# The last output tile of a gated attention and MLP kernel: two engines for its scaling, two queues for its stores

## The chip, the core and the metric

The kernel runs on one core of a Trainium2 chip. The metric is the device time of one execution in microseconds. A profile's span, from the first to the last instruction, is slightly shorter than the time of the same execution (268.4 us where the time was 270.24 us). The engines are TensorE (PE; PEld is its weight load), VectorE (DVE), ScalarE (ACT), GpSimd (POOL) and SyncE (SP). SPq and ACTq are the sequencers of SyncE and ScalarE, where DMAs are issued.

In this text, **tail** is the time from the end of the last matmul to the end of the span, and **relative times** ("at -0.43 us") are counted from the end of that last matmul. Both are read from the trace's instruction and semaphore records, which are finer than the rounded lines of the views.

## The reference

Two branches work on the same input x of 2048 x 512 (bfloat16), and a sigmoid gate per row mixes them:

```python
g = sigmoid((x * gate_w).sum(-1, keepdims=True))
a = attention_with_memory(x, wq, wk, wv, beta) @ wo    # 32 heads, 4 segments of 512 rows
h = gelu(x @ w_gate) * (x @ w_up)                       # 512 -> 1792
b = h @ w_down                                          # 1792 -> 512
return g * a + (1 - g) * b
```

## The kernel before

The kernel has a list scheduler of its own that orders all tasks on the engines before anything is emitted. Only the end matters here. The output is made in tiles of 128 rows x 512 columns. For each tile TensorE adds up the MLP part (`wdn`) and the attention part (`wo`) in one PSUM bank, one engine scales it by a factor per row into an SBUF buffer, and a DMA stores that buffer. The buffers come from a ring, `osb`, of two. The very last tile is cut in two column groups so that the last piece of work after TensorE is small: 384 columns first (in a buffer of the same ring), then 128 columns (in a buffer of its own, `ose`).

```python
RINGS = {..., "osb": 2, "ose": 1}
...
def out_group(s, qt, prio, cols=slice(0, D)):
    part = (cols.stop - cols.start) / D
    ring = "osb" if part > 1 / 4 else "ose"
    ...                                    # TensorE: 14 steps of wdn, 4 of wo
    def fo(e):
        bx["o"] = rtile(ring, [P, D if ring == "osb" else P])
        f = omz[:, s, qt:qt + 1]
        if e == "ACT":
            nc.scalar.activation(bx["o"][:, oc], bank(first)[:, cols], AF.Copy, scale=f)
        else:
            nc.vector.tensor_scalar_mul(bx["o"][:, oc], bank(first)[:, cols], f)
    ev = add(["DVE", "ACT"], [130 + 530 * part, 155 + 430 * part], fo, deps=[g, TAB["omz"]],
             alloc=[ring], frees=[("gen", first)])
    add("SP", 600, lambda _: nc.sync.dma_start(out2[q0:q0 + P, cols], bx["o"][:, oc]),
        deps=[ev], frees=[(ring, ev)], lat=2000)
...
for qt in range(KT - 1):                                       # three whole tiles
    out_group(NSEG - 1, qt, 9000 + qt)
for h, cols in enumerate((slice(0, 3 * P), slice(3 * P, D))):  # 384, then 128 columns
    out_group(NSEG - 1, KT - 1, 9010 + h, cols)
```

The scheduler chose ScalarE for all of the last four tiles. So the 384-column group takes the buffer that the tile two before it used, and has to wait until that tile's store has landed.

The softmax here doesn't subtract the row's maximum and nothing guards it: scores larger than these inputs give would overflow.

Of the kernel before, what the change touches and what calls it, by code (L numbers as in the profile page):

```python
# [13 lines left out]
P = 128  # L14
# [45 lines left out]
class Sched:  # L60
# [15 lines left out]
    def add(self, engs, cost, fn, **kw):  # L76

        if "PE" in engs and 0 < kw["prio"] < 9000:
            kw["prio"] += (ord(next(self.shift, "M")) - ord("M")) / 2
        engs = {engs: cost} if isinstance(engs, str) else dict(zip(engs, cost))  # L80
        t = Task(engs, fn, **kw)
        t.seq = len(self.tasks)
        self.tasks.append(t)
        return t
# [207 lines left out]
def kernel(  # L292
# [15 lines left out]
    nc = tc.nc  # L308
    assert tuple(A_x.shape) == (1, NSEG * L, D)
    x2 = A_x[0]  # L310
    out2 = out[0]
# [17 lines left out]
    add = S.add  # L329

    def ctile(name, shape, dtype=BF):
        return cp.tile(shape, dtype, name=name, tag=name)
# [10 lines left out]
    def bank(t, i=0):  # L343
        return banks(t, "gen", i)[:, 0, :]
# [4 lines left out]
    def rtile(ring, shape, dtype=BF, pool=None):  # L349
        pool = pool or (pools["wp"] if ring in WP else rp)  # L350
        return pool.tile(shape, dtype, name=ring, tag=ring, bufs=RINGS[ring])
# [21 lines left out]
    omz = ctile("omz", [P, NSEG, KT], F32)  # L373
# [86 lines left out]
    def group(name, cost, mms, prio, deps, alloc="gen", also=None, **kw):  # L460

        box = {}

        def fn(e):
            box["t"] = pair(t) if alloc == "pair" else bank(t)
            if also:
                also[1]()
            mms(box["t"])
        t = add("PE", cost, fn, prio=prio, deps=deps, alloc=[alloc] + ([also[0]] if also else []),
                **kw)  # L470
        return t, box
# [19 lines left out]
    def dense(t, lhsT, rhs, start, stop):  # L491


        if not tiled:
            nc.tensor.matmul(t, lhsT=lhsT, rhs=rhs, start=start, stop=stop)  # L495
            return
        for j in range(4):
            a = slice(32 * j, 32 * j + 32)
            nc.tensor.matmul(t[a, :], lhsT=lhsT[:, a], rhs=rhs, start=start, stop=stop,  # L499
                             tile_position=(0, 32 * j), skip_group_check=True)  # L500
# [141 lines left out]
    TAB = {}  # L642
# [100 lines left out]
    for s in range(NSEG):  # L743
        for hp in range(HS // 2):
            gate_pair(s, hp, -959 + 20 * s + hp)
            if s == 1 and hp == HS // 2 - 1:
                g, box = group("bps", 60, f_bps, -922, [a_be])
# [299 lines left out]
    def out_group(s, qt, prio, cols=slice(0, D)):  # L1047


        late = s == NSEG - 1  # L1050
        att = [t_wo] + [OTT[(s, c)] for c in range(NCH)]
        part = (cols.stop - cols.start) / D
        ring = "osb" if part > 1 / 4 else "ose"
        oc = cols if ring == "osb" else slice(0, P)
        q0 = s * L + qt * P
        prev = first = None
        for lo in range(0, HS, 2):
            def fn(_, lo=lo):
                for hs in (lo, lo + 1):
                    dense(bank(first)[:, cols], G[:, s, hs, qt * P:(qt + 1) * P], wdn[:, hs, cols],  # L1060
                          hs == 0, False)
            prev = add("PE", 2 * MM * part, fn, prio=prio, mode="more" if lo else "open",
                       deps=[prev] if lo else [UPT[(s, hs)] for hs in range(HS)] + [TAB["wdn"]]
                       + ([] if late else att[:ATT]), alloc=[] if lo else ["gen"], final=late)
            first = first or prev

        def fn_o(_):
            for c in range(NCH):
                dense(bank(first)[:, cols], xT[:, c, q0:q0 + P], wo[:, c, cols], False,
                      c == NCH - 1)  # L1070
        g = add("PE", 4 * MM * part, fn_o, prio=prio, deps=[prev] + att, final=late, mode="more")
        bx = {}
# [5 lines that stand above are left out]
                nc.scalar.activation(bx["o"][:, oc], bank(first)[:, cols], AF.Copy, scale=f)  # L1078
            else:
                nc.vector.tensor_scalar_mul(bx["o"][:, oc], bank(first)[:, cols], f)  # L1080
        ev = add(["DVE", "ACT"], [130 + 530 * part, 155 + 430 * part], fo, deps=[g, TAB["omz"]],
                 alloc=[ring], frees=[("gen", first)])
        add("SP", 600, lambda _: nc.sync.dma_start(out2[q0:q0 + P, cols], bx["o"][:, oc]),
            deps=[ev], frees=[(ring, ev)], lat=2000)

    TAB["first_x"] = None
# [4 lines left out]
    def fillers(s):  # L1091


        AE = ["DVE", "ACT"]
        n0 = NSLOT * s
        n1 = n0 + NSLOT
        if s > 0:
            mem_den(s, n0 + 2)
            for gp in range(2):
                mem_num(s, gp, n0 + 3 + 4 * gp)  # L1100
        ph = 2.5
        if s < NSEG - 1:
            phi_k(s, 0, ph)
            for pr in range(2):
                for which in "kq":
                    for c in (2 * pr, 2 * pr + 1):
                        qk_group(s + 1, c, which, n1 - 10 + 1.5 * c, AE)
                phi_q(s + 1, pr, ph)
                if pr == 0:
                    phi_k(s, 1, ph)  # L1110
            for i in range(KT):
                v_group(s + 1, i, n1 - 3, AE)
            for pr in range(2):
                m_update(s, pr, n1 - 8 + 5 * pr)
        for i, x in enumerate(UPS[s]):
            up_group(*x, n0 + 4 + 16 * (i + 1) / len(UPS[s]))
        if s > 0:
            for qt in range(KT):
                out_group(s - 1, qt, n0 + 5 * qt + 5)
# [12 lines left out]
    for qt in range(KT - 1):  # L1132
        out_group(NSEG - 1, qt, 9000 + qt)
    for h, cols in enumerate((slice(0, 3 * P), slice(3 * P, D))):
        out_group(NSEG - 1, KT - 1, 9010 + h, cols)
# [30 lines left out]
```

## Time and profile before

The time was 269.78 us, the median of three runs (269.45 to 270.19). From the page of the profile before: the span, the busy time of each engine with its share of the span, and the chain of waits by engine.

```profile
span 268.4 us, 10277 instructions
## 1 busy us (share of the span) xinstructions
PE 263.8 (98%) x4546; PEld 126.0 (47%) x4546; DVE 173.8 (65%) x354; ACT 213.1 (79%) x237; POOL 114.8 (43%) x205
...
## 4 chain that ended last, share of the span: by engine, by line
PE 94%; DMA 3%; ACT 1%; SPq 0%; issue 0%; ACTq 0%
...
```

TensorE is busy for 98% of the span and makes up 94% of the chain of waits. A change that leaves TensorE's instructions alone can only change what comes after its last one. The next fence is the timeline of the kernel before over that end: start, duration (both in us), engine, line, operation, output<-inputs, and in brackets how long the engine had been idle and what ended the wait.

```profile
...
261.75 3.99 SPq L1083 DMA_DIRECT2D out_dram<-osb  x3
...
263.30 0.82 PE L499 MATMUL ps<-wo,xT 128*32 128x384 bf16 x16
...
264.73 0.40 PE L499 MATMUL ps<-wo,xT 128*32 128x128 bf16 x16
264.80 0.58 ACT L1078 ACTIVATE osb<-ps,omz 128x384 bf16<-128x384 f32 x1 [1.42 <-DMA out_dram<-osb]
265.28 0.36 ACT L1078 ACTIVATE ose<-ps,omz 128x128 bf16<-128x128 f32 x1
265.83 0.38 SPq L1083 DMA_DIRECT2D out_dram<-ose  x1
```

How to read it. TensorE is done with the 384 columns at 263.30 + 0.82 = 264.12 us, but ScalarE starts to scale them only at 264.80; the bracket says that it sat idle for 1.42 us and that a store from `osb` ended the wait. The 128 columns are done at 264.73 + 0.40 = 265.13, and ScalarE starts on them at 265.28. Their store is issued at 265.83, behind the 384-column store on SyncE. In numbers from the trace's records (the landing of a store shows there as sixteen steps of a semaphore, called its sixteen parts here):

| kernel before, first profile | at (us of the span) | relative to the last matmul's end |
|---|---|---|
| last matmul ends | 265.13 | 0 |
| 15 of 16 parts of the store that frees the buffer have landed | 263.46 | -1.67 |
| its last part has landed (called **S** below) | 264.70 | -0.43 |
| ScalarE on 384 columns | 264.80 to 265.38 | -0.33 to +0.25 |
| ScalarE on 128 columns | 265.28 to 265.64 | +0.15 to +0.51 |
| SyncE issues the 384-column, the 128-column store | 265.41, 265.83 | +0.28, +0.70 |
| these stores have landed | 267.04, 267.34 | +1.91, +2.22 |
| end of the span (closing waits and barrier: 1.04) | 268.38 | +3.25 = the tail |

### The profile page before, as it was taken

To read this page: it belongs to the slowest core of one execution; us is meant where nothing else is said; L and a number is where in the kernel's file an instruction comes from. 1 tells how busy PE (TensorE), PEld (TensorE's weight loads), DVE (VectorE), ACT (ScalarE), POOL (GpSimd) and SP (SyncE) were. 2 spreads that over 40 slices of the span, in tenths; PEclk is the share of its full clock that TensorE was granted. 3 is DMA by queue.
4 is the path that set the end of the run, shared out by engine and by line. 5 is a ranking of instruction groups with operands and counts; after the bars stand their busy time and mean duration, and the time that the engine had idled before them with its cause. 6 is when DMAs were issued, how large, how long until landed. Compare 5 with 4: busy or idle time off the path is not lost.

```text
span 268.4 us, 10277 instructions
## 1 busy us (share of the span) xinstructions
PE 263.8 (98%) x4546; PEld 126.0 (47%) x4546; DVE 173.8 (65%) x354; ACT 213.1 (79%) x237; POOL 114.8 (43%) x205
## 2 busy tenths in 40 slices
PE   8999999999999999999999999999999999999995
PEld 5644444444444554444444444444454444444453
DVE  1440392070788999898869788969668886464450
ACT  3446665556989998999889888999999898989612
POOL 8100000031346454558454655566555474455710
PEclk9999999999999999999999999999999999999999
DMA  6994627325022041100002120000000000000002
GB/s 217 345 145 102 189 61 253 118 93 188 2 42 43 2 42 22 23 4 5 2 22 21 44 61 22 2 2 4 22 24 22 22 4 4 22 22 22 22 2 81
DMA packets 23764, 15.73 MB, mean 59 GB/s; under 512 B 14120, under 2 KB 22696, under 8 KB 23720
## 3 DMA queue, kind: packets, MB, share of 16 engines
q1 hardware_dynamic: 23016, 14.42, 21.4%
q8 instruction: 35, 0.57, 0.9%
q10 hardware_dynamic: 704, 0.66, 0.7%
q14 instruction: 9, 0.07, 0.1%
HBM read 9.83 MB, written 2.10 MB: 44 GB/s over the span
## 4 chain that ended last, share of the span: by engine, by line
PE 94%; DMA 3%; ACT 1%; SPq 0%; issue 0%; ACTq 0%
PE ps L499 54%; PE ps L495 21%; PE ps L790 10%; PE ps L836 7%; DMA wk<-in_A_wk_dram 2%; PE ps L595 1%; DMA out_dram<-osb 1%; ACT pT L807 1%; PE ps L943 1%; PE ps L1022 1%; ACT osb L1078 0%; SPq L400 0%; PE ps L983 0%; PE ps L577 0%; ACT qT L317 0%
## 5 line engine op out<-in xcount | busy, mean ns | idle before, releaser
L807 ACT ACTIVATE pT<-ps 128x1024 bf16<-128x1024 f32 x160 | 153.8, 1026 | 11.2 <-PE ps L790 9.0
L816 POOL TENSOR_SCALAR_AFFINE_SELECT pT<-pT 128x512 bf16<-128x512 bf16 (+1 forms) x160 | 92.2, 577 | 89.0 <-ACT pT L807 88.6
L499 PE MATMUL ps<-wdn,G 128*32 128x512 bf16 (+2 forms) x952 | 60.0, 368 | 0.1
L499 PE MATMUL ps<-xT,wup 128*32 128x512 bf16 x896 | 56.2, 380 | 0.0
L708 DVE TENSOR_TENSOR G<-ps,G 128x512 bf16<-128x512 f32 x56 | 37.9, 681 | 16.9 <-PE ps L499 16.6
L495 PE MATMUL ps<-xT,wga 128*128 128x512 bf16 x224 | 48.5, 379 | 0.0
L698 ACT ACTIVATE G<-ps 128x1024 bf16<-128x1024 f32 x28 | 28.7, 1024 | 22.2 <-PE ps L495 21.5
L495 PEld LDWEIGHTS <-wga 128*128 128x128 bf16 x224 | 21.9, 98 | 26.3
L499 PEld LDWEIGHTS <-wup 128*32 128x32 bf16 x896 | 22.6, 96 | 22.0 <-issue 4.0
L854 DVE STREAM_TRANSPOSE T<-ps 128x512 f32<-128x512 f32 x32 | 22.6, 706 | 15.1 <-PE ps L836 15.1
L499 PEld LDWEIGHTS <-G 128*32 128x32 bf16 x952 | 21.4, 96 | 19.8 <-issue 4.0
L651 DVE SCALAR_TENSOR_TENSOR zs<-wdn 128x512 f32<-128x512 bf16 x16 | 11.1, 691 | 26.2 <-DMA wdn<-in_gate_w_dram 13.7
L671 POOL COPY G_87<-omz 32x16 f32<-32x16 f32 x16 | 3.5, 219 | 50.1 <-DVE zs L651 49.5
L790 PE MATMUL ps<-qT,kT 16*128 16x256 bf16 (+2 forms) x320 | 17.3, 274 | 0.0
L790 PE MATMUL ps<-qT,kO 32*128 32x128 bf16 (+2 forms) x320 | 17.3, 272 | 0.0
L499 PEld LDWEIGHTS <-xT 128*32 128x32 bf16 x464 | 11.8, 97 | 10.7 <-issue 0.7
L499 PE MATMUL ps<-wo,xT 128*32 128x512 bf16 (+2 forms) x272 | 16.5, 367 | 0.0
L790 PEld LDWEIGHTS <-kT 16*128 16x128 bf16 x320 | 6.8, 92 | 19.2 <-issue 19.0
L1078 ACT ACTIVATE osb<-ps,omz 128x512 bf16<-128x512 f32 (+1 forms) x10 | 6.8, 677 | 10.2 <-PE ps L499 7.7
L1039 POOL TENSOR_TENSOR Nm<-Tm,rm 128x512 bf16<-128x512 f32 x12 | 13.1, 1092 | 0.7 <-DVE N L877 0.7
L790 PEld LDWEIGHTS <-kO 32*128 32x128 bf16 x320 | 6.9, 92 | 12.4 <-issue 12.3
L499 PE MATMUL ps<-xT,wq 128*32 128x512 bf16 x192 | 12.4, 380 | 0.1
(97 smaller groups left out, 259.2 us busy)
## 6 DMA issues: line engine op xcount, KB each, us to landing
out_dram<-osb SPq DMA_DIRECT2D x15, 128.0 KB
wup<-in_B_w_up_dram SPq DMA_DIRECT2D x1, 1792.0 KB
wdn<-in_B_w_down_dram SPq DMA_DIRECT2D x1, 1792.0 KB
wdn<-in_A_x_dram SPq DMA_DIRECT2D x3, 512.0 KB
wga<-in_B_w_gate_dram SPq DMA_DIRECT2D x1, 1280.0 KB
wga<-in_B_w_gate_dram SPq DMA_DIRECT2D x1, 512.0 KB
wv<-in_A_wv_dram SPq DMA_DIRECT2D x1, 512.0 KB
wo<-in_A_wo_dram SPq DMA_DIRECT2D x16, 32.0 KB
```

Of the source, the lines that this page charges most:

```text
L495: nc.tensor.matmul(t, lhsT=lhsT, rhs=rhs, start=start, stop=stop)
L499: nc.tensor.matmul(t[a, :], lhsT=lhsT[:, a], rhs=rhs, start=start, stop=stop, tile_position=(0, 32 * j), skip_group_check=True)
L651: nc.vector.scalar_tensor_tensor(out=zs[:, :], in0=row, scalar=1.0, in1=gwB, op0=ALU.mult, op1=ALU.mult, accum_out=omz[:, s, kt:kt + 1])
L698: ge = evac("ACT", g, box, lambda e, t: nc.scalar.activation(dst, t[:, :, :], AF.Gelu_apprx_tanh), cost=920, ring="pair")
L708: UPT[(s, hs)] = evac("DVE", g, box, lambda e, t: nc.vector.tensor_mul(G[:, s, hs, :], t[:, :], G[:, s, hs, :]))
L790: nc.tensor.matmul(A[j // 2][:, j % 2, at * P:(at + nq) * P], lhsT=l, rhs=r, start=True, stop=True, tile_position=(32 * j, 0))
L807: nc.scalar.activation(pT[(s, t, h)][:, :, :], A[h][:, :, :], AF.Exp, scale=0.25)
L816: nc.gpsimd.affine_select(out=v, in_=v, pattern=pat, compare_op=ALU.is_ge, fill=0.0, base=0, channel_multiplier=-1)
L836: nc.tensor.matmul(t[32 * q:32 * q + 32, qb * P:(qb + nq) * P], lhsT=vz[s % 2][:, kt, h * VW:h * VW + 32], rhs=pT[(s, t0 + w, j // 2)][:, ...
L854: nc.vector.transpose(TT[key][:, e, :, :].rearrange("p a b -> p (a b)"), t[:, :])
L1039: nc.gpsimd.tensor_mul(NMt[(s, c)][:, :, :, :], bx[i][:, :, :, :], RMt[s][:, :, 2 * c:2 * c + 2][:, :, :, None] .to_broadcast((P, QB, 2, DH)))
L1078: nc.scalar.activation(bx["o"][:, oc], bank(first)[:, cols], AF.Copy, scale=f)
```

## The change

It wants the two last scalings to run side by side, and the two last stores to be issued side by side: the 384 columns are scaled by VectorE, the 128 columns by ScalarE, and ScalarE issues the 128-column store itself, right behind its scaling.

```diff
-        ev = add(["DVE", "ACT"], [130 + 530 * part, 155 + 430 * part], fo, deps=[g, TAB["omz"]],
-                 alloc=[ring], frees=[("gen", first)])
-        add("SP", 600, lambda _: nc.sync.dma_start(out2[q0:q0 + P, cols], bx["o"][:, oc]),
+        engs = ["DVE", "ACT"] if part == 1 else ["DVE"] if part > .5 else ["ACT"]
+        ev = add(engs, [130 + 530 * part if e == "DVE" else 155 + 430 * part for e in engs], fo,
+                 deps=[g, TAB["omz"]], alloc=[ring], frees=[("gen", first)])
+        q = nc.sync if ring == "osb" else nc.scalar
+        add("SP", 600, lambda _: q.dma_start(out2[q0:q0 + P, cols], bx["o"][:, oc]),
             deps=[ev], frees=[(ring, ev)], lat=2000)
```

In the built program, TensorE's instructions stand in the same order in both kernels; on the other engines only these last instructions move.

## The prediction

> **What bounds the kernel now.** TensorE: it is busy 263.8 us of a 268.4 us span (98%, busy table); the chain of waits is 94% TensorE. The change leaves TensorE's instruction order as it was (9094 rows), and on the other engines only the last output tile's instructions move. So all that can change is the tail after TensorE's last matmul ends (265.13 us in the timeline): 3.25 us, 1.2% of the span.
>
> **The tail before, from the trace.**
> - TensorE finishes the 384-column group at about 264.12 us, but its ScalarE scaling starts only at 264.80: it waits for a buffer of the two-deep osb ring, freed by the store issued at 261.75. Fifteen of that store's sixteen completion steps came by 263.46, the last at 264.70; a 16 KB packet of the instruction queue ran from 262.23 to 263.54 and, I think, held it up.
> - ScalarE: 384 columns 264.80 to 265.38 (580 ns), 128 columns 265.28 to 265.64 (359 ns).
> - SyncE issues the 384-column store at 265.41 (0.33 us), the 128-column store at 265.83 (0.38 us). They complete at 267.04 and 267.34, 1.63 and 1.51 us after issue. From the last completion to the end of the span it is 1.04 us of closing waits and barrier.
>
> **What the change does.**
> 1. The 384 columns go to VectorE. It waits for the same buffer, so starts at 264.80 too. Its 128x512 form took 748 ns in six calls (by-form groups); with about 1 ns per column (its casts: 418 ns for 256 columns, 678 for 512) I estimate 615 ns, 35 ns more than ScalarE. Store issue about 265.44, completion about 267.07: no gain here.
> 2. The 128 columns no longer share ScalarE. They can start when TensorE is done, about 265.20 instead of 265.28: 0.05 to 0.1 us.
> 3. Their store is issued by ScalarE at about 265.59, not 265.83 behind SyncE's other issue. The Trainium skill, "DMA: Bandwidth & Descriptors", section "Issuing engines are not separate DMA queues", says that issuing on several engines "will only save the time on the sequencer it takes to initiate the DMA". The trace agrees in size: 0.33 us, plus 0.09 us to the next. Completion about 267.10 to 267.20, packets interleaved with the 384-column store's.
>
> **On the critical path:** the last completion moves from 267.34 to about 267.15: 0.2 us, 0.07% of the time, below the spread of the runs before (269.45 to 270.19).
>
> **Predicted time: 269.6 us** (8 in 10: 269.1 to 270.1). Chance of faster by over 2%: 0.005; within 2%: 0.99; slower: 0.005.
>
> **What would show each step:**
> - Timeline of the last 4 us: VectorE's scaling of 128x384 starting at 264.7 to 264.9 and taking 0.58 to 0.65 us; ScalarE's 128x128 starting at 265.15 to 265.25; a ScalarE-queue DMA issue near 265.6, before or within 0.2 us after SyncE's.
> - Both stores landing within 0.2 us of each other, span 268.1 to 268.3.
> - Waits: VectorE's last instruction waits for the store of osb, not for TensorE. If it waits for TensorE, the late completion step was chance.
>
> **What would make it wrong:** a ScalarE-queue store that is slower to start after 250 us of rest, or two issuers that slow each other (loss up to 0.5 us); a late completion step that falls elsewhere (shift of about 0.5 us either way); a longer closing sequence because two queues have to be drained. A difference of 2% could only come from TensorE's clock or the chip.

## The result and the profile after

The changed kernel took 270.02 us, the median of six runs (269.83 to 270.32). The kernel before, in six runs with them, took 270.31 us (269.45 to 271.06). The ratio is 0.9993, with a 95% interval of 0.9972 to 1.0014: the same. A ratio here is the mean time of one kernel's fast runs over that of the other's of the same rounds, so it is not quite the ratio of the medians quoted beside it. Scaled to the six-run median of the kernel before, 0.9993 x 270.31 = 270.12 us, just above the predicted range; the median of 270.02 itself lies just inside it.

The one profile looks like a success. The timeline of the changed kernel over its end:

```profile
...
264.48 0.62 DVE L1080 TENSOR_SCALAR osb<-ps,omz 128x384 bf16<-128x384 f32 x1 [5.54 <-DMA out_dram<-osb]
...
264.63 0.40 PE L499 MATMUL ps<-wo,xT 128*32 128x128 bf16 x16
265.08 0.37 ACT L1078 ACTIVATE ose<-ps,omz 128x128 bf16<-128x128 f32 x1 [1.75 <-PE ps L499]
265.48 0.36 ACTq L1085 DMA_DIRECT2D out_dram<-ose  x1
```

And the waits of the changed kernel over its last microseconds (who waited for what: us in total, times, longest):

```profile
...
DVE osb L1080 <- DMA out_dram<-osb: 5.5, 1, 5.5
ACT ose L1078 <- PE ps L499: 1.7, 1, 1.7
...
```

VectorE waited for the store, as predicted, and took 0.62 us. It started at 264.48, though, earlier than the 264.7 to 264.9 of the prediction's first check. ScalarE now waited for TensorE alone and started 0.05 us after the last matmul; it issued its store at +0.45 instead of +0.70. The span is 268.01 instead of 268.38 us (predicted 268.1 to 268.3), and the tail 2.98 instead of 3.25 us. Taking the spans apart: of the 0.37 us, 0.27 lie in the tail. 0.09 lie before the 46th weight load of TensorE (7.73 instead of 7.83 us), where nothing was changed; the stretch from there to the last matmul took 257.29 us here and 257.30 us before.

But one entry does not belong to the change. The store that frees VectorE's buffer completed at S = -0.74 us here and at -0.43 in the profile before. It was issued at the same relative time, -3.38, in both, and 15 of its 16 parts had landed at -1.67 in both. In both, one 16 KB packet of the instruction queue began 0.5 us after the issue; it lasted 1.30 us before and 0.98 us after, and the late part landed 1.16 and 1.15 us after the packet's end. So the two profiles differ by a draw of luck as well as by the change, and the question is how much of the 0.27 us is which.

### The profile page after: what moved, and what is told of

Read it like the earlier page. It is cut to its first block, busy times and chain, and to the rows that moved or that the text cites. A ratio compares the mean times of both kernels' runs of the same rounds, so it can differ in the third digit from the quotient of the medians.

```text
span 268.0 us, 10270 instructions
## 1 busy us (share of the span) xinstructions
PE 263.6 (98%) x4540; PEld 125.8 (47%) x4546; DVE 174.5 (65%) x355; ACT 212.7 (79%) x236; POOL 114.8 (43%) x205
## 4 chain that ended last, share of the span: by engine, by line
PE 98%; ACT 1%; issue 0%
PE ps L499 56%; PE ps L495 21%; PE ps L790 10%; PE ps L836 7%; PE ps L595 1%; PE ps L551 1%; PE ps L577 1%; ACT pT L807 1%; PE ps L943 1%; PE ps L1022 1%; PE ps L983 0%; ACT qT L317 0%; ACT ose L1078 0%; PE ps L604 0%; PE ps L720 0%
## 5 line engine op out<-in xcount | busy, mean ns | idle before, releaser
L1078 ACT ACTIVATE osb<-ps,omz 128x512 bf16<-128x512 f32 x9 | 6.2, 689 | 8.8 <-PE ps L499 7.7
```

## The experiments

Theory A: the time of the tail is decided by S, the late end of one store, because it holds back the 384 columns, and through them (on a shared engine or a shared queue) the 128 columns. The lateness comes from an instruction packet. With an early S, the kernel before loses nothing by sharing an engine and a queue, and the change gains nothing.

Theory B, the rival and the intent of the change: sharing ScalarE and SyncE costs about 0.27 us by itself; in one variant it is the engine that counts.

Every run below gave correct results. Its profile gives the tail to a few ns; its times cannot, since single runs of one kernel spread by 0.3% and more. Relative times in us of all fourteen profiles:

| run | packet starts, lasts | S | 384 columns start | 128 columns start | 128-column store issued, landed | tail |
|---|---|---|---|---|---|---|
| before, first profile | -2.89, 1.30 | -0.43 | -0.33 | +0.15 | +0.70, +2.22 | 3.25 |
| after, first profile | -2.88, 0.98 | -0.74 | -0.55 | +0.05 | +0.45, +1.95 | 2.98 |
| c_before | -2.88, 0.92 | -0.77 | -0.66 | +0.06 | +0.45, +1.89 | 2.92 |
| c_after | -2.48, 0.95 | -0.37 | -0.17 | +0.05 | +0.45, +2.36 | 3.39 |
| e1_engines_only | -3.23, 1.30 | -0.40 | -0.21 | +0.05 | +1.02, +2.53 | 3.57 |
| e2_queue_only | -2.83, 1.07 | -0.55 | -0.44 | +0.06 | +0.45, +1.97 | 3.00 |
| e3_before_own_buffer | -3.13, 1.27 | -0.37 (not waited for) | +0.01 | +0.48 | +1.04, +2.56 | 3.59 |
| e4_after_own_buffer | -3.10, 1.04 | -0.61 (not waited for) | -0.95 | +0.05 | +0.45, +2.22 | 3.25 |
| e5_before_shifted_fetch | -4.84, 1.22 and +0.23, 0.95 | -1.67 | -0.90 | +0.05 | +0.45, +2.65 | 3.67 |
| e9_after_shifted_fetch | -4.99, 1.02 and +0.07, 0.93 | -1.68 | -0.89 | +0.05 | +0.45, +2.29 | 3.33 |
| e10_before_shift192 | -0.88, 0.93 | -1.67 | -0.90 | +0.05 | +0.45, +1.89 | 2.92 |
| e11_after_shift192 | -1.65, 1.24 | -1.67 | -0.89 | +0.05 | +0.45, +1.93 | 2.95 |
| e12_before_two_buffers | -2.92, 1.35 | -0.43 (not waited for) | -0.95 | +0.05 | +0.45, +1.89 | 2.92 |
| e13_after_two_buffers | -3.20, 1.66 | +0.01 (not waited for) | -0.95 | +0.05 | +0.45, +1.93 | 2.95 |

The records of single DMA packets, which the views of the profile leave out, tie the late part to the instruction packet. In the first profile of the kernel before, the packet ends at -1.59. The late part is eight packets of 1 KB: the first starts at -1.60, they run one after another, and a packet of 4 bytes follows them at -0.91. In all fourteen profiles, the eight packets of the first late part start within 0.06 us of the instruction packet's end, and that part lands 1.10 to 1.23 us after this end. So when S is late, it follows from when the packet starts and how long it lasts. In the ten profiles without extra matmuls (e5, e9, e10 and e11 have them), where the packet started at -3.10 or earlier (e1, e3, e4, e13), it caught two stores, and the second one's part landed 0.3 us after the first one's; where it started between -2.92 and -2.48, it caught one.

### The same two kernels once more

No edit. What was expected of the kernel before:

> The kernel before once more, against itself: a null test of the timing and a second look at its tail (from the end of the last matmul to the end of the span; 3.25 us in the first profile). Theory A (the wait for the buffer decides): the late completion of the store that frees the buffer, S, was 0.43 us before the end of the last matmul in the first profile of before, but 0.74 us before it in the profile of after, where the 16 KB instruction packet was shorter (0.98 instead of 1.30 us). If S comes here at -0.43 again, the tail is 3.25; if it comes at -0.74, ScalarE is free in time and SyncE's issues don't queue, and the tail is 2.98, as in after. Theory B (sharing ScalarE and SyncE costs 0.27 us by itself): 3.25 whatever S is. The ratio of times should be 1.000 within 0.002; single runs spread by 0.3% or more, which is more than the effect of the change.

Its timeline over the end:

```profile
...
264.88 0.58 ACT L1078 ACTIVATE osb<-ps,omz 128x384 bf16<-128x384 f32 x1 [1.08 <-DMA out_dram<-osb]
...
265.59 0.37 ACT L1078 ACTIVATE ose<-ps,omz 128x128 bf16<-128x128 f32 x1
265.99 0.33 SPq L1083 DMA_DIRECT2D out_dram<-ose  x1
```

The last matmul ended at 265.54 us. The packet was short, S was -0.77, and the unchanged kernel had a tail of 2.92 us, shorter than that of the changed one. Its time was 270.28 us, ratio to itself 1.0010 (0.9993 to 1.0027).

What was expected of the changed kernel:

> The changed kernel once more. Theory A: with S at -0.74 us the tail is 2.98 us, set by the 128-column store; with S at -0.43 VectorE's 384 columns end at +0.38, their store completes at about +2.04 and the tail is 3.1 to 3.15, so the change is worth about 0.1 us at an equal S, and nothing at an early S. Theory B: 2.98 whatever S is. Time within 0.2% of the kernel before on this chip; both may lie anywhere from 269.4 to 271.

And its timeline over the end:

```profile
...
265.33 0.62 DVE L1080 TENSOR_SCALAR osb<-ps,omz 128x384 bf16<-128x384 f32 x1 [5.91 <-DMA out_dram<-osb]
265.56 0.37 ACT L1078 ACTIVATE ose<-ps,omz 128x128 bf16<-128x128 f32 x1 [1.75 <-PE ps L499]
265.96 0.39 ACTq L1085 DMA_DIRECT2D out_dram<-ose  x1
```

The last matmul ended at 265.50 us. The packet began 0.4 us later than in the three profiles above, S was -0.37, and the changed kernel had a tail of 3.39 us. Its time was 270.23 us, ratio 1.0014 (1.0001 to 1.0027). So each kernel has short and long tails: 2.92 and 3.25 before, 2.98 and 3.39 after. At a nearly equal S (-0.77 and -0.74; -0.43 and -0.37) the changed kernel's tail is the longer one by 0.07 and 0.14 us, part of which is its slightly later S. This is against theory B. Theory A's 3.1 to 3.15 for a late S was too short, though. The two stores were issued 0.02 us apart, by SyncE and by ScalarE, and ScalarE's took 1.91 us from issue to landing, where it had taken 1.49 us in the first profile. The later S came with a later packet: it lasted only 0.95 us but ended at -1.53.

### Half of the change: the engines alone

This edit and the next are shown against the changed kernel.

```diff
-        q = nc.sync if ring == "osb" else nc.scalar
+        q = nc.sync
```

> 384 columns on VectorE, 128 on ScalarE, but both stores issued by SyncE as before. Theory A: the 128-column store queues behind the 384-column issue: issued at S+1.26 us after the last matmul's end, or at +0.45 if that is later; with S from -0.74 to -0.43 that is a tail of 3.06 to 3.37 us, so no better than before or even worse by 0.1, as VectorE is slower on 384 columns. Theory B, engines variant (what counts is that two engines scale at once): 2.98.

The timeline of this run over its end (the first line is the last but one tile):

```profile
...
264.73 0.69 ACT L1078 ACTIVATE osb<-ps,omz 128x512 bf16<-128x512 f32 x1 [2.81 <-DMA out_dram<-osb]
...
265.38 0.37 ACT L1078 ACTIVATE ose<-ps,omz 128x128 bf16<-128x128 f32 x1
266.34 0.41 SPq L1085 DMA_DIRECT2D out_dram<-ose  x1
```

The tail was 3.57 us (time 270.62, ratio 1.0027, 1.0009 to 1.0044). The 128 columns were ready on time, at +0.42, and their store was issued at +1.02, third in SyncE's queue. This time the packet had caught two stores: the tile before (first line) also got its buffer late. With engines alone there is no gain in this profile. The miss of 0.2 us over the expected 3.06 to 3.37 goes with this second late store, which the expectation had not reckoned with: it put a third issue into SyncE's queue.

### The other half: the queue alone

```diff
-        engs = ["DVE", "ACT"] if part == 1 else ["DVE"] if part > .5 else ["ACT"]
+        engs = ["DVE", "ACT"] if part == 1 else ["ACT"]
```

> Both scalings on ScalarE as before, only the 128-column store moved to ScalarE's queue. Theory A: ScalarE starts the 128 columns at S+0.58 or +0.05 us, whichever is later; with S from -0.74 to -0.43 the tail is 2.98 to 3.08 us: nearly all of the gain comes with the queue alone. Theory B, engines variant: 3.25, as in before.

The timeline of this run over its end:

```profile
...
264.54 0.58 ACT L1078 ACTIVATE osb<-ps,omz 128x384 bf16<-128x384 f32 x1 [1.26 <-DMA out_dram<-osb]
...
265.04 0.37 ACT L1078 ACTIVATE ose<-ps,omz 128x128 bf16<-128x128 f32 x1
...
```

The last matmul ended at 264.98 us. The tail was 3.00 us with S at -0.55 (time 270.40, ratio 1.0019, 0.9999 to 1.0038). ScalarE did both scalings and still began the 128 columns 0.06 us after the last matmul. VectorE is not needed for a short tail. The reading for the queue is weaker: with S at -0.55, by the durations of the profile before, SyncE would have issued the second store at about S + 1.13 = +0.58 instead of +0.45.

### No wait for the last buffer

One weight tile, `wq`, is long dead by the end; SBUF has no room for another buffer (a build with one of 384 columns asked for 0.5 KB a partition too much). The 384 columns go there, so that they wait for no store. The first run does this to the kernel before, with ScalarE and SyncE kept, the second to the changed one.

```diff
-        ring = "osb" if part > 1 / 4 else "ose"
+        ring = "osb" if part == 1 else "spare" if cols.start == 0 else "ose"
+        held = [] if ring == "spare" else [ring]          # replaces [ring] in alloc and frees
...
-            bx["o"] = rtile(ring, ...)
+            bx["o"] = wq[:, 0, :] if ring == "spare" else rtile(ring, ...)
```

The comment is not in the code. Left out are the column range inside the buffer and, in the first run, a line that keeps the 384 and 128 columns on ScalarE.

> The kernel before, with one thing changed: the 384 columns are scaled into a weight tile that is long dead, not into the two-deep osb ring, so they wait for no store. Engines and queues as before (ScalarE, SyncE). Theory A: ScalarE starts the 384 columns when TensorE ends that group, 0.9 to 1.0 us before the last matmul's end, and the 128 columns at +0.05; the 128-column store is issued at +0.45 and the tail is 2.92 us, as in the second run of before, wherever the instruction packet falls for that store (it may still hold up the tile before: then up to 3.1). Theory B (sharing an engine and a queue costs by itself): 3.25.

> The changed kernel with the same dead weight tile for the 384 columns. Theory A: VectorE starts them 0.9 to 1.0 us before the last matmul's end; the 128-column store is issued by ScalarE at +0.45 and the tail is 2.95 to 3.0 us, no better than with ScalarE and SyncE alone. Theory B: clearly shorter than the kernel before with its own buffer, by 0.1 us or more.

The timeline over the end, first of the kernel before with the spare buffer:

```profile
...
264.36 0.69 ACT L1079 ACTIVATE osb<-ps,omz 128x512 bf16<-128x512 f32 x1 [2.83 <-DMA out_dram<-osb]
...
264.95 0.57 ACT L1079 ACTIVATE wq<-ps,omz 128x384 bf16<-128x384 f32 x1
265.41 0.37 ACT L1079 ACTIVATE ose<-ps,omz 128x128 bf16<-128x128 f32 x1
...
```

The same view of the changed kernel with it:

```profile
...
264.26 0.62 DVE L1081 TENSOR_SCALAR wq<-ps,omz 128x384 bf16<-128x384 f32 x1 [5.14 <-PE ps L499]
264.41 0.69 ACT L1079 ACTIVATE osb<-ps,omz 128x512 bf16<-128x512 f32 x1 [2.60 <-DMA out_dram<-osb]
...
265.27 0.37 ACT L1079 ACTIVATE ose<-ps,omz 128x128 bf16<-128x128 f32 x1 [0.17 <-PE ps L499]
...
```

Both expectations failed: the tails were 3.59 and 3.25 us (times 270.00 and 270.37, ratios 0.9997 and 1.0008, both the same within their intervals). In these two runs the packet started earlier, at -3.13 and -3.10, and caught the store of one tile earlier as well, whose last part landed at -0.68 and -0.91. The last but one tile waited for that (2.83 and 2.60 us idle). In the first of the two runs, it stands before the 384 columns in ScalarE's order, and these, ready at -1, had to wait behind it. In the second, VectorE passed it by, and only the queues suffered: SyncE issued the 384-column store at +0.33, 0.12 us before ScalarE's.

The edit did not cause this wait. In e1_engines_only, without a spare buffer, the packet started at -3.23 and the same tile sat idle for 2.81 us; with a later packet it waits too, but only for about 1 us (0.97 in the first profile). So the pair does not test theory A; it shows that one buffer leaves the wait of the tile before, which the draw of the packet can make long. It also suggests where a second engine helps: when ScalarE is held up. But of the 0.34 us between the two tails, 0.24 are the draw (-0.68 against -0.91), so by this estimate about 0.1 us is left for the engine.

### Moving the packet

The trace holds 35 packets of 16 KB on the instruction queue q8, most of them 232 to 280 TensorE instructions apart, 256 on average over the second half of the span. If they are TensorE's instruction fetches, more TensorE instructions early on move the last packet forward in the tail. 16 gate matmuls of the first segment, early in the span, were written in the four-column-tile form that the kernel uses later anyway. That is 96 instructions more and no other change; the first run does it to the kernel before, the second to the changed one.

```diff
         def mms(t):
+            if s == 0 and hp < 2:
+                tiled.append(None)
             for i in range(2):
                 mm_x(t[:, i, :], wga, (2 * hp + i) * P, s)
+            if s == 0 and hp < 2:
+                tiled.pop()
```

> The kernel before, with 96 more TensorE instructions early on (16 gate matmuls in the four-column-tile form that the kernel uses later), nothing changed in the tail. If the 16 KB packets are TensorE's instructions, one for every 256, the last one comes 96 instructions, some 2.4 us, earlier (at about -5.3 us instead of -2.9 to -2.5) and meets none of the last stores. Theory A: the store that frees the buffer then completes as its other 15 parts do, at about -1.67 us; ScalarE starts the 384 columns at -0.9 to -1.0; the tail is 2.92 us. If the packet has nothing to do with the late completion, S stays at -0.4 to -0.8.

> The changed kernel with the same 96 instructions. Theory A: tail 2.95 to 3.0 us, equal to or 0.05 us longer than that of the kernel before with the shifted packet: without the late completion the change gains nothing. Theory B: 0.2 us or more shorter than the latter. The times of both should be within 0.2% of each other.

The instruction queue in the DMA view of the kernel before, as it was (packets, MB, share of 16 engines):

```profile
...
q8 instruction: 35, 0.57, 0.9%
...
```

And shifted:

```profile
...
q8 instruction: 36, 0.59, 0.9%
...
```

The end of the shifted kernel before in the timeline:

```profile
...
264.40 0.58 ACT L1082 ACTIVATE osb<-ps,omz 128x384 bf16<-128x384 f32 x1 [0.75 <-PE ps L499]
...
265.75 1.09 SPq L1087 DMA_DIRECT2D out_dram<-ose  x1
```

And the end of the shifted changed kernel:

```profile
...
264.35 0.62 DVE L1084 TENSOR_SCALAR osb<-ps,omz 128x384 bf16<-128x384 f32 x1 [5.20 <-PE ps L499]
...
265.69 0.37 ACTq L1089 DMA_DIRECT2D out_dram<-ose  x1
```

The first half of the expectation held in both. The packet began at -4.84 and -4.99, S was -1.67 and -1.68, and the 384 columns now waited for TensorE, not for a store. With the packet gone, the late part of that store was gone. But a 36th packet appeared, at +0.23 and +0.07, on top of the last stores, and made one of their 16 parts late instead: in the first run the 384-column store had 15 parts by +1.35 and the last at +2.29. The tails were 3.67 and 3.33 us, so the expected 2.92 and 2.95 to 3.0 were missed, and the times rose to 271.15 and 270.59 us (ratios 1.0038, 1.0023 to 1.0053, and 1.0023, 1.0006 to 1.0041). Part of that is the 16 rewritten matmuls themselves: the stretch from the 46th weight load to the last matmul is 257.52 instead of 257.30 us. The changed kernel was the better by 0.34 us in this case: with the packet in the way, SyncE's issue of the second store took 1.09 us instead of 0.33 or 0.38, while ScalarE's took 0.37. This suggests that here a queue of its own paid, but one pair does not show it. The packets ended at +1.18 and +1.00, so 0.19 of the 0.34 us are the draw. And a running packet does not always hold up an issue: SyncE's issues that began during one took 1.31 and 1.35 us in e12 and e13, but 0.50 in the first profile and 0.33 in c_after and e10, so ScalarE's 0.37 may be luck.

The second try uses 32 gate matmuls (`hp < 4`), 192 instructions more, so that the packets fall where nothing in the tail waits for the store that they hit.

> The kernel before with 192 more TensorE instructions early on instead of 96 (32 gate matmuls in the four-column-tile form). The shift by 96 freed the buffer early but let one more 16 KB packet start at +0.1 to +0.2 us, on top of the last stores. By the spacing of 256 instructions, the packets should now start at about -7.5 and -1.5 to -1.0 us, where only the store of the last but one tile is in flight, for which nothing in the tail waits. Theory A: S at -1.67, 384 columns from -0.95 to -0.89, all 16 completion steps of each last store close together, tail 2.92 us, the shortest that this kernel can have with its split. Theory B: 3.25 also without any packet in the way.

> The changed kernel with the same 192 instructions. Theory A: tail 2.95 to 3.0 us, that is 0.03 to 0.08 us longer than the kernel before with this shift, since ScalarE's issue was slower by 0.03 to 0.05 us so far. Theory B: shorter than it by 0.2 us or more. Times within 0.2% of each other.

The timeline over the end of the kernel before with this shift:

```profile
...
264.69 0.58 ACT L1082 ACTIVATE osb<-ps,omz 128x384 bf16<-128x384 f32 x1 [0.84 <-PE ps L499]
...
266.04 0.33 SPq L1087 DMA_DIRECT2D out_dram<-ose  x1
```

And of the changed kernel with it:

```profile
...
264.33 0.62 DVE L1084 TENSOR_SCALAR osb<-ps,omz 128x384 bf16<-128x384 f32 x1 [5.20 <-PE ps L499]
...
265.68 0.36 ACTq L1089 DMA_DIRECT2D out_dram<-ose  x1
```

The packet fell at -0.88 and -1.65 and made the store of the last but one tile late (last part at +1.28 where the other 15 were in at -0.01, in the first run), and nothing waited for that. The tails were 2.92 us for the kernel before and 2.95 us for the changed one. Without an ill-placed packet, sharing ScalarE and SyncE costs nothing, and the change loses 0.03 us (one profile each): the 128-column store is issued at +0.45 in both, and lands 1.44 us later from SyncE and 1.48 us later from ScalarE. The 32 rewritten matmuls cost 0.22 us themselves, as much as the 16 did (the same stretch is again 257.52 us), so the times, 270.31 and 270.25 us (ratios 1.0003 and 1.0009), gain nothing.

### No wait in the tail at all

The packet stays where it was, but the last but one tile and the 384 columns both go to dead weight tiles.

```diff
-        ring = "osb" if part == 1 else "spare" if cols.start == 0 else "ose"
+        ring = ("spare" if late and cols.start == 0 and qt >= KT - 2 else
+                "osb" if part == 1 else "ose")
...
-            bx["o"] = wq[:, 0, :] if ring == "spare" else rtile(ring, ...)
+            bx["o"] = wq[:, qt - 2, :] if ring == "spare" else rtile(ring, ...)
```

`late` is true for the last segment. Left out are the same lines as for one buffer.

> The kernel before; the last but one tile and the 384 columns are both scaled into dead weight tiles, so that no scaling of the tail waits for a store (with one such buffer, the tile before still waited, and kept ScalarE from the 384 columns in the order of its queue). The packet stays where it is. Theory A: ScalarE does the last but one tile at about -3.2 us, the 384 columns at -0.95, the 128 columns at +0.05; tail 2.92 us in spite of the packet. Theory B: 3.25.

> The changed kernel with the same two dead weight tiles. Theory A: tail 2.95 to 3.0 us; the change adds nothing once no scaling waits for a store. Theory B: at least 0.1 us shorter than the kernel before with two buffers.

The timeline over the end of the kernel before with two buffers:

```profile
...
262.18 0.69 ACT L1080 ACTIVATE wq<-ps,omz 128x512 bf16<-128x512 f32 x1 [0.18 <-PE ps L499]
...
264.46 0.58 ACT L1080 ACTIVATE wq<-ps,omz 128x384 bf16<-128x384 f32 x1 [1.59 <-PE ps L499]
...
265.46 0.37 ACT L1080 ACTIVATE ose<-ps,omz 128x128 bf16<-128x128 f32 x1 [0.42 <-PE ps L499]
265.86 0.33 SPq L1087 DMA_DIRECT2D out_dram<-ose  x1
```

And of the changed kernel with them:

```profile
...
263.93 0.62 DVE L1082 TENSOR_SCALAR wq<-ps,omz 128x384 bf16<-128x384 f32 x1 [5.14 <-PE ps L499]
...
265.33 0.36 ACTq L1087 DMA_DIRECT2D out_dram<-ose  x1
```

The packet was there, with 1.35 and 1.66 us the longest in any tail, and the old stores' last parts landed as late as -0.43 and +0.01. No scaling waited for them: each bracket now names TensorE. The tails were 2.92 and 2.95 us, as with the shifted packet, and again the kernel before is ahead by 0.03 us. Two quite different ways to take the late store out of the way give the same two tails. The times were 269.92 us (ratio 0.9993, 0.9979 to 1.0006) and 270.12 us (1.0001, 0.9986 to 1.0016). The kernel before with two buffers has the lowest median of all kernels in these comparisons (the first three runs of the kernel before, 269.78, apart) and keeps its short tail when the packet is long, but the times do not separate it from the kernel before.

## Why the prediction was right or wrong

Right: that TensorE bounds the kernel and that only the tail can change; that the difference stays far below 2%; that VectorE waits for the store of `osb` and takes 0.62 us (615 ns estimated); that ScalarE starts the 128 columns right after the last matmul (0.07 us predicted, 0.05 measured); that its issue comes at about 265.59 - 265.13 = +0.46 (measured +0.45 in every run of the changed kernel); and that an instruction packet was behind the late part of the store.

Wrong are the base of the sum (the first point), which put the forecast too low, and the step that makes the change worth 0.2 us (the second and third), which took one draw for the kernel. That the ratio of 0.9993, some -0.19 us, is so near to the predicted -0.2 is luck: its interval runs from -0.76 to +0.38 us, and the second comparison gave 1.0014, +0.38 us.

- **"Predicted time: 269.6 us (8 in 10: 269.1 to 270.1)".** The forecast was a base less a gain of 0.2 us, and the mis-sized term is the base, the median of three runs, 269.78. With three more runs the median of the same kernel was 270.31, 0.53 us higher; in three later comparisons of eleven runs each it was 270.00, 270.21 and 270.08 us. Its single runs went from 269.36 to 271.06. The changed kernel took 270.02 in one and 270.23 in another comparison. The range (1.0 us) was little wider than the spread of three runs (0.74), and it was centred below their median, which was itself on the low side. Where the spread comes from can be read: in the ten profiles without extra matmuls, the stretch from the 46th weight load to the last matmul is 257.29 to 257.30 us each time. The start before it varies from 7.58 to 8.24 us, with TensorE waiting for the loads of x and `wk` there, and the tail of the two kernels as given from 2.92 to 3.39. These two add up to more than a microsecond of spread, against an effect of 0.2.
- **"It waits for the same buffer, so starts at 264.80 too"**, that is, taking S from one profile as a property of the kernel. S was -0.43, -0.74, -0.77 and -0.37 in four profiles of the two kernels. The prediction named this risk ("a late completion step that falls elsewhere") but compared both kernels at one fixed S, that of a long packet.
- **"the last completion moves from 267.34 to about 267.15: 0.2 us".** In the first pair of profiles the tail did shrink by 0.27, for the wrong reason. With S out of play the term is -0.03 us, a small loss (2.92 against 2.95, twice). The 0.24 us by which the prediction moved the issue of the last store (265.83 to 265.59, up to 0.1 us of it from ScalarE, the rest from SyncE's queue) were real in that pair, 0.25 us measured. But both parts were consequences of the late S; with an early S the kernel before issues at +0.45 as well (c_before, e10_before_shift192, e12_before_two_buffers).
- **"Completion about 267.10 to 267.20, packets interleaved"**, priced as free. From its issue to its landing, ScalarE's store took 1.48 us when SyncE's was issued 0.70 us earlier (e11_after_shift192), 1.49 at 0.35 (after), 1.52 at 0.29 (e2_queue_only), 1.77 at 0.12 (e4_after_own_buffer) and 1.91 when both came within 0.02 us (c_after). So just when a late S makes the queue an issue, the two stores land later. The prediction had named this risk ("two issuers that slow each other") but given it no place in the sum.

Still open: the trace does not name the DMA engine that a packet ran on, so that the instruction packet and the late part were on one of them remains inferred. The inference is close: the late part follows the packet to whichever store is in flight (e5, e9, e10, e11), and its own packets start where the instruction packet ends, in every profile. Also open is why the packet's start and length vary (in the tails of the profiles without extra matmuls -3.23 to -2.48, and 0.92 to 1.66 us), and whether a second queue escapes a packet that holds up the first.

## What to carry to other kernels

Before two profiles are compared in a tail of a few microseconds, line them up at the last matmul and ask of each wait whether it is the kernel's or a draw. Here a store that was complete but for one of its sixteen parts was a draw, and a second profile of the unchanged kernel showed it. What took the wait out of the tail was a buffer that nobody has to give back, for the last two tiles and not only the last, rather than a second engine or queue behind the same wait; the times of six runs were too coarse to show either. And a forecast range must be at least as wide as the spread of medians of the unchanged kernel, which three runs do not show.

## What the Trainium skill lacked or had wrong

- "Runtime: NRT & Kernel Launch", section "Instruction fetch mechanics", says that instructions are refilled in 16 KiB blocks of 256 and that the cost of crossing a block is "mostly hidden". The trace agrees on the blocks: 35 packets of 16,384 bytes for TensorE's 9,092 recorded matmuls and weight loads, and a 36th with 96 more. It lacks that the fetch is not hidden from other DMAs: a packet took 0.9 to 1.8 us, and one of the sixteen parts of a store in flight landed up to 2.2 us after the other fifteen (1.24 us in the first profile).
- "DMA: Bandwidth & Descriptors", section "Queues, rings and completion order", says that a DMA engine takes turns between its queues packet by packet. It does not say how long a turn of the instruction queue is: 0.9 to 1.8 us here, against about 0.05 us for a 1 KB packet of a store. A reader of that page cannot foresee how late the part will be. That the two share an engine is inferred here, from the late part's packets, which start within 0.06 us of the instruction packet's end in all fourteen profiles.
- The same page, section "Issuing engines are not separate DMA queues", says that issuing from several engines only saves the time of the sequencer, "which is usually small relative to the DMA itself". The saving agrees in the ordinary case (0.33 to 0.38 us for an issue). Two things are missing: issued within 0.02 us of each other, the second queue's store took 1.91 us instead of 1.48; and an issue can be held up while an instruction packet runs (SyncE's took 1.09 to 1.35 us in e5, e12 and e13, but 0.33 in c_after and e10; ScalarE's took 0.37 in its one case, e9).
- "CRC Debugging", section "Comparing the Two Runs", names queue 14 for the instruction refills. In this trace the packets that come once for 256 TensorE instructions are on q8 (35 of 16 KB); q14, which the DMA view calls an instruction queue too, holds nine packets, none of 16 KB; what they carry is not shown here.
